# First two chunks of a gated delta rule as one pair with raw keys, two-bank PSUM tiles moved whole, squares summed on ScalarE

## The chip, the cores and the metric

The kernel runs on one core of one Trainium2 chip. The metric is the device time of one execution in microseconds. The core has TensorE (PE, with weight loads listed apart as PEld), VectorE (DVE), ScalarE (ACT), GpSimd (POOL) and SyncE (SP), each with its own queue of instructions, worked off in order; they wait for one another by semaphores.

## The reference

A gated delta rule over 768 time steps for 4 batches x 8 heads with head size 48, and then a dense layer pair with softplus between:

```python
k_n = k / (np.linalg.norm(k, axis=-1, keepdims=True) + 1e-06)
for t in range(S):                                   # state: B, H, 48, 48
    readout = np.einsum('bhd,bhde->bhe', q[:, :, t], state)
    y[:, :, t] = g[:, :, t] * readout
    v_old = np.einsum('bhde,bhd->bhe', state, kt)
    state = state + bt[:, :, :, None] * np.einsum('bhd,bhe->bhde', kt, vt - v_old)
...
x = y.transpose(0, 2, 1, 3).reshape(3072, 384)
h = x @ w_in                                         # 384 -> 2048
g = np.maximum(h, 0.0) + np.log1p(np.exp(-np.abs(h)))
return g @ w_out                                     # 2048 -> 384
```

## The kernel before

The 768 steps are cut into 12 chunks of 64. Within a chunk the recurrence becomes matrix products of 64 x 64 blocks for each of the 32 batch-head pairs: a triangular system in the chunk's keys is inverted, and the states follow from chunk to chunk.

*Items and order.* The kernel does not issue instructions as it goes. It records items (a kind, a chunk, the engines that may run it, what it needs, which tiles it uses) and then emits them in an order written out as a table, `_ORDER`: a word such as `D171` puts item 171 on VectorE. A tile of a ring is taken when the first item that uses it is emitted, and freed after the last. So the table fixes the order on every engine and in SyncE's queue of loads and stores, and it fixes which buffer a chunk gets.

*Stages of a chunk.*
- `norms`: squares of the keys (line 346), their sums by a reduction on VectorE (line 352), the root (ScalarE up to chunk 2, POOL's power after that, line 363), the added 1e-6 and the reciprocal. Chunk 0 is *raw*: its keys go on without being scaled, and the norm is put into beta (`lbeta`) and into v (line 783) instead.
- `front`: keys scaled (`kmul`, line 396) or cast, transposed on TensorE (line 412), evicted (`kev`), queries likewise (line 444, `qev`), then the products of keys with keys and queries (`gram`, line 506). Each comes out in two PSUM banks, m = 0 and 1; four instructions take it out: `kkc` (keys, through the helper of lines 209 and 213) and `mask` (line 488).
- `inverse`: for a group of chunks. Groups are chunk 0, chunk 1, and then pairs. A transpose of 32 x 32 blocks (lines 560 and 565), fifteen elimination steps of two small instructions each (lines 611 and 618) on VectorE or POOL, scalings by the mask of a pair (`ca`, `cb`), transposes back (line 661 for a pair, 665 for one chunk), `tx` (a swap of partition halves) and three products with evictions between (lines 691, 715, 736: `xs`, `td2`, `z`).
- `chain`: old state times keys (`ks`, line 773), v minus that (`w`, line 804), product with the inverse (`umm`, line 818, evicted as `u1`), a second product (`zu`, line 831, `u2`), the new state (`smm`, line 848, `s` at 862), outputs (`qs`, `ymm` line 874, `y` line 888), and a transpose into `xt`.
- `dense`: line 927 makes h in PSUM (two tiles), line 939 takes softplus on ScalarE, line 954 multiplies with w_out, `o` copies out, stores follow. These stand between the chunk stages on TensorE.

Filler matmuls (line 984) on the identity stand in gaps at the start. The PSUM rings are `d` (five single banks), `h` (two) and `o` (one):

```python
r_w = ring("w16", 3, [P, H, D], F16)
r_u = ring("u16", 6, [P, H, D], F16)
r_s = ring("s16", 5, [P, H, D], F16)
p_d = ring("d", 5, [P, 512], F32, psum)
p_h = ring("h", 2, [P, 512], F32, psum)
p_o = ring("o", 1, [P, 512], F32, psum)
```

A stage that makes two banks takes two `d` tiles; one item each takes them out, on ScalarE or VectorE as the table says.

## Time and profile before

| what | us |
|---|---|
| median of 3 runs | 252.6 (252.19 to 253.89) |
| the profiled execution | 250.61 |
| its span, first to last instruction | 248.9 |
| TensorE busy | 219.2 (88%) |
| VectorE busy | 173.0 (69%) |
| ScalarE busy | 160.0 (64%) |
| POOL busy | 107.7 (43%) |

The profile is of one execution. A row of a group gives the line, engine, operation, tiles (written <- read) and shapes, how often, the busy time, the mean of one in ns, and the idle time of the engine ahead of it with what ended it. In the view by windows, each engine has its busy time in that stretch and in brackets its instructions, then come the granted TensorE clock, the DMA share and the traffic. A row of the timeline gives start, duration, engine, line and operation, and in square brackets an idle time and what ended it.

### The profile page before, as it was taken

Reading aid. Unit: us, or ns where it says so; the run is one execution under the profiler, and the core shown is the slowest. Engines: PE = TensorE matmul, PEld = TensorE weight load, DVE = VectorE, ACT = ScalarE, POOL = GpSimd, SP = SyncE. Lnnn points to the kernel's source line nnn. Section 1 sums busy time; section 2 is a strip of 40 time slices with the busy share of each in tenths; the row PEclk is TensorE's granted clock in tenths of the full one; section 3 lists DMA queues with packets and bytes.
Section 4 is the critical chain, followed back from the end, with each engine's and each line's share of the span. In section 5 each row is a group of like instructions: output and inputs, shape, how many; then the busy total and the mean of one; then the engine's idle time right before and its main releaser. Section 6 shows DMA issues by size and latency. Waiting matters only on the chain.

```text
span 248.9 us, 11162 instructions
## 1 busy us (share of the span) xinstructions
PE 219.2 (88%) x4880; PEld 136.6 (55%) x4880; DVE 173.0 (69%) x414; ACT 160.0 (64%) x305; POOL 107.7 (43%) x183
## 2 busy tenths in 40 slices
PE   7666059857998998999999999999999999999993
PEld 2243055644775665455765566655566455677751
DVE  3969999964599987997899989988887233711000
ACT  7675668854596788998668677466672665235540
POOL 8546999662286827858769353303110000000000
PEclk9799657996899999999999999999999999999999
DMA  7999899999996379630999221498300430022013
GB/s 104 185 238 167 115 201 154 203 185 183 208 154 121 71 142 181 169 63 6 172 168 152 41 69 37 91 151 130 66 22 18 97 85 13 5 48 49 18 48 95
DMA packets 86832, 27.55 MB, mean 111 GB/s; under 512 B 77056, under 2 KB 86784, under 8 KB 86784
## 3 DMA queue, kind: packets, MB, share of 16 engines
q1 hardware_dynamic: 81824, 22.31, 52.8%
q0 software_dynamic: 3840, 3.16, 8.6%
q10 hardware_dynamic: 1120, 1.38, 2.2%
q8 instruction: 38, 0.62, 1.1%
q14 instruction: 10, 0.08, 0.2%
HBM read 25.26 MB, written 4.72 MB: 120 GB/s over the span
## 4 chain that ended last, share of the span: by engine, by line
PE 68%; DVE 12%; issue 6%; ACT 6%; DMA 3%; POOL 2%; SPq 1%; POOLq 0%; DVEq 0%; ACTq 0%
PE o L954 25%; PE h L927 21%; PE d L773 3%; ACT kqt L209 2%; PE d L874 2%; PE d L506 2%; PE d L818 2%; DVE tt L618 2%; PE d L444 2%; PE d L831 2%; DMA f<-in_k_dram 2%; DVE tmp L611 2%; DVE mt L488 2%; DVE nv L352 2%; DMA f<-in_q_dram 2%
## 5 line engine op out<-in xcount | busy, mean ns | idle before, releaser
L954 PE MATMUL o<-w_out,ga 128*128 128x384 f16 x384 | 78.3, 329 | 1.1 <-ACT osb L209 0.6
L927 PE MATMUL h<-xt,w_in 128*128 128x512 f16 (+1 forms) x384 | 75.1, 331 | 0.6 <-ACT ga L939 0.5
L939 ACT ACTIVATE ga<-h 128x512 f16<-128x512 f32 x96 | 56.9, 600 | 28.7 <-PE h L927 26.3
L927 PEld LDWEIGHTS <-w_in 128*128 128x128 f16 x384 | 35.5, 99 | 21.6 <-issue 1.1
L954 PEld LDWEIGHTS <-ga 128*128 128x128 f16 x384 | 33.8, 98 | 21.7 <-issue 2.0
L611 POOL TENSOR_TENSOR tmp<-nn,tt 128x78 f32<-128x78 f32 (+7 forms) x57 | 21.5, 377 | 37.2 <-DVE tt L618 32.3
L363 POOL TENSOR_TENSOR nv<-nv,half_c 128x16 f32<-128x16 f32 x9 | 26.3, 2920 | 2.2 <-DVE nv L352 2.2
L618 POOL TENSOR_TENSOR tt<-tt,tmp 128x78 f32<-128x78 f32 (+7 forms) x57 | 20.5, 360 | 4.5
L209 ACT ACTIVATE kqt<-d 128x1024 f16<-128x1024 f16 (+1 forms) x21 | 19.1, 945 | 4.3 <-PE d L412 2.1
L396 POOL TENSOR_TENSOR kn<-f,nv 128x768 f16<-128x768 f32 (+1 forms) x10 | 14.4, 1445 | 13.2 <-PE d L848 6.9
L209 ACT ACTIVATE u<-d 128x384 f16<-128x384 f32 x31 | 14.3, 491 | 9.0 <-PE d L818 4.4
L488 DVE TENSOR_TENSOR mt<-d,mask 128x256 f16<-128x256 f32 x48 | 18.3, 412 | 1.9 <-ACT kk L209 1.0
L209 ACT ACTIVATE osb<-o 128x384 f32<-128x384 f32 x20 | 9.8, 490 | 14.0 <-PE o L954 13.6
L506 PE MATMUL d<-kqt 48*64 48x128 f16 (+1 forms) x448 | 11.3, 217 | 6.7 <-ACT kqt L209 3.2
L888 DVE TENSOR_TENSOR yg<-d,f 128x384 f16<-128x384 f32 x24 | 12.3, 548 | 5.6 <-PE d L874 5.4
L211 DVE CAST u<-d 128x384 f16<-128x384 f32 x17 | 9.3, 554 | 9.3 <-PE d L818 6.6
L984 PE MATMUL h<-ident 128*128 128x512 f16 x40 | 14.0, 513 | 1.7 <-DVE ident L197 1.7
L804 DVE TENSOR_TENSOR w<-f,d 128x384 f16<-128x384 f32 x22 | 11.8, 546 | 4.0 <-PE d L773 4.0
L618 DVE TENSOR_TENSOR tt<-tt,tmp 128x110 f32<-128x110 f32 (+7 forms) x48 | 13.2, 274 | 1.6
L506 PEld LDWEIGHTS <-kqt 48*64 48x64 f16 x448 | 7.6, 109 | 12.2 <-issue 6.8
L611 DVE TENSOR_TENSOR tmp<-nn,tt 128x110 f32<-128x110 f32 (+7 forms) x48 | 12.9, 269 | 1.7 <-POOL tt L618 0.6
L209 ACT ACTIVATE kk<-d 128x256 f16<-128x256 f32 x37 | 12.3, 385 | 2.7 <-PE d L506 2.3
(115 smaller groups left out, 340.4 us busy)
## 6 DMA issues: line engine op xcount, KB each, us to landing
f<-in_k_dram SPq DMA_DIRECT2D x24, 192.0 KB, 5.9
f<-in_q_dram SPq DMA_DIRECT2D x24, 192.0 KB, 4.7
f<-in_v_dram SPq DMA_DIRECT2D x24, 192.0 KB, 5.8
f<-in_g_dram SPq DMA_DIRECT2D x24, 192.0 KB, 5.3
out_dram<-osb SPq DMA_DIRECT2D x34, 96.0 KB, 2.2
w_in<-in_moe_w_in_dram POOLq DMA_DIRECT2D x4, 384.0 KB, 7.2
w_out<-in_moe_w_out_dram POOLq DMA_DIRECT2D x4, 384.0 KB, 8.1
out_dram<-osb ACTq DMA_DIRECT2D x14, 96.0 KB, 2.5
```

Source lines behind the costliest of these rows:

```text
L209: nc.scalar.activation(o, x, AF.Copy, scale=float(sign))
L363: lambda en: nc.gpsimd.tensor_tensor(nv.ap[:, :NU], nv.ap[:, :NU], half_c[:, :NU], ALU.pow),
L396: ENG[en].tensor_tensor(kn[c].ap[:, sl, :, :D], kf.ap[:, sl], nv.ap[:, :NU].rearrange("p (a h) -> p a h", a=2)[:, sl, :, None] .broadcast_ ...
L488: nc.vector.tensor_tensor(mt[c][m].ap[:, NP * p : NP * p + NP], gb[m].ap.rearrange("p (i b) -> p i b", i=NP)[:, :, n : n + C], mask[:, Non ...
L506: nc.tensor.matmul(gb[m].ap.rearrange("p (i b) -> p i b", i=NP)[HALF[r], i, lo:hi], x[:, :C], x[:, lo:hi],)
L611: ENG[en].tensor_tensor(t, nn.ap[:, :, j : j + 1, j + 1 :].broadcast_to([P, 2, w, n]), tt.ap[:, :, :w, j : j + 1].broadcast_to([P, 2, w, n ...
L618: ENG[en].tensor_tensor(rows, rows, t, ALU.add)
L888: lambda en, m=m: nc.vector.tensor_tensor(heads(yg.ap, m), hd(yp[m].ap), heads(gf.ap, m), ALU.mult),
L927: nc.tensor.matmul(hp.ap[:, n * b : n * b + n], w_in[:, j, f * P : (f + 1) * P], xt.ap[:, j, t0 : t0 + n], start=(j == 0), stop=(j == 2),)
L939: lambda en, hp=hp, o=gb: nc.scalar.activation(o.ap, hp.ap, AF.Softplus),
L954: nc.tensor.matmul(op.ap[:, :DM], b.ap[:, col + c0 : col + c0 + 128], w_out[:, f, :], start=(f == 0), stop=(f == NF - 1),)
L984: nc.tensor.matmul(hp.ap, ident, ident[:, None, :].broadcast_to([P, 4, P]))
```

## The change

- Groups are now pairs throughout: chunks 0 and 1 are the first pair, both with raw keys. `lbeta` takes both norms at once, so one inverse less is run (six in place of seven). v of chunk 0 is scaled as part of `w0`; v of chunk 1 as chunk 0's was.
- Roots of chunks 0 to 3 on ScalarE (before: 0 to 2); where POOL takes the root it also adds 1e-6.
- A `d` tile has two banks, and there are two of them; a new single-bank ring `e` serves the transposes. From chunk 2 on (`N_APART`) one instruction takes both banks out; chunks 0 and 1 keep one for each bank.
- `xs` is cut by column block and not by bank, scales by a per-partition mask value, and may run on ScalarE.
- For chunks 9 and 11 (`SUMMED`) squares and sums are made by sixteen ScalarE instructions with an accumulated output, without the reduction on VectorE. Keys may be scaled on ScalarE by sixteen instructions too; the new order does so for chunk 9.
- The identity in f32 borrows another tile, beta for the first pair is loaded without clearing the tile, and the order is a new one (1140 words in place of 1276).

```diff
-N_RAW = 1
-N_SQRT = 3
+N_RAW = 2
+N_SQRT = 4
 N_SPLIT = 2
-GROUPS = [[0], [1], [2, 3], [4, 5], [6, 7], [8, 9], [10, 11]]
+GROUPS = [[0, 1], [2, 3], [4, 5], [6, 7], [8, 9], [10, 11]]
+N_APART = 2
+SUMMED = (9, 11)
+N_LONE = 2
...
-    p_d = ring("d", 5, [P, 512], F32, psum)
+    p_d = ring("d", 2, [P, 1024], F32, psum)
+    p_e = ring("e", 1, [P, 512], F32, psum)
...
+    def moved(kind, c, tag, engs, fn, deps, bufs, size):
+        cuts = [slice(0, 2)] if c >= N_APART else [slice(0, 1), slice(1, 2)]
+        return [
+            add(kind, tag + (f".{rs.start}" if len(cuts) > 1 else ""), engs,
+                lambda en, rs=rs: fn(en, rs), deps=deps, bufs=bufs,
+                size=size * (rs.stop - rs.start))
+            for rs in cuts]
...
+        def summed(en):
+            for a in range(2):
+                for h in range(H):
+                    nc.scalar.activation(
+                        ksq.ap[:, a, h], kf.ap[:, a, h], AF.Square,
+                        accum_out=nv.ap[:, H * a + h : H * a + h + 1])
+
+        if c in SUMMED:
+            i2 = add("sqa", f"{c}", "A", summed, deps=kl, bufs=[kf, ksq, nv], size=768)
...
+            def root(en):
+                nc.gpsimd.tensor_tensor(nvs(), nvs(), half_c[:, :NU], ALU.pow)
+                nc.gpsimd.tensor_scalar_add(nvs(), nvs(), 1e-6)
...
+                    if en == "A":
+                        for a in range(sl.start, sl.stop):
+                            for h in range(H):
+                                nc.scalar.activation(
+                                    kn[c].ap[:, a, h, :D], kf.ap[:, a, h], AF.Copy,
+                                    scale=nv.ap[:, H * a + h : H * a + h + 1])
+                        return
...
-        a4 = [add("u1", f"{c}.{r}", "AD", lambda en, r=r: copy(en, u1[r].ap, hd(up[r].ap)),
-                  deps=[a3], bufs=[u1[r], up[r]], size=384) for r in range(2)]
+        a4 = moved("u1", c, f"{c}", "AD", lambda en, rs: copy(en, u1.ap[:, rs], hds(up, rs)),
+                   [a3], [u1, up], 384)
```

`kkc`, `mask`, `td2`, `z`, `w`, `u2`, `s` and `y` change in the same way as `u1`.

More of the change, by code (lines that the diff above doesn't have):

```diff
@@ L174 @@
     nc.scalar.activation(dummy, half_c[:, :1], AF.Sqrt)
+    ident32 = r_tmp.tiles[1]
     make_identity(nc, ident32)
-    nc.gpsimd.memset(beta_l[:, :2], 0.0)
     for r in range(2):
@@ L244 @@
         for r_ in (r_kn, r_qn):
-            for t in r_.tiles[n : n + 1]:
+            for t in r_.tiles[n : n + 1] if r_ is r_qn or n > 1 else []:
                 setup[n].append(
@@ L341, in norms @@
         kf, kl = tiles["k", c]
-        ksq, nv = Buf(r_f), Buf(r_nv)
+        ksq = Buf(r_f)
+        if RAW[c] and c % 2:
+            nv = nv_of[c - 1]
+        else:
+            nv = Buf(r_nv)
         def square(en):
@@ L893, in chain @@
         xt = xts[cc]
[L894 removed]
+        ytp = Buf(p_e)
         def ytr(en):
@@ L997 @@
         chain(c)
-    jobs = [[0], [1]] + [[c, c + 1] for c in range(2, NC - 2, 2)] + [[NC - 2], [NC - 1]]
+    jobs = [[c] for c in range(N_LONE)]
+    jobs += [[c, c + 1] for c in range(N_LONE, NC - 2, 2)] + [[NC - 2], [NC - 1]]
     for cs in jobs:
```

459 lines of the change are left out of this document (223 added, 236 removed).

## The prediction

> **What bounds the kernel now.** I read the page first: busy shares, slices of the span, and the chain that ended last.
>
> ```profile
> span 248.9 us, 11162 instructions
> PE 219.2 (88%) x4880; PEld 136.6 (55%) x4880; DVE 173.0 (69%) x414; ACT 160.0 (64%) x305; POOL 107.7 (43%) x183
> PE   7666059857998998999999999999999999999993
> PEclk9799657996899999999999999999999999999999
> PE 68%; DVE 12%; issue 6%; ACT 6%; DMA 3%; POOL 2%; SPq 1%; POOLq 0%; DVEq 0%; ACTq 0%
> ```
>
> TensorE is busy for 88% of the span, and the chain that ended last runs over it for 68%. Its slices hold nines and a few eights from the eleventh on (62 us); what is not full lies ahead of that. So the end is set by how early TensorE is given work without gaps, and then by the work itself, which the change leaves alone (4880 matmuls before and after, ten filler groups among them in both).
>
> To see where the head start is made I cut the span at the first matmul of line 818 (the product with the inverse) of chunks 0, 1, 2, 3, 6 and 11. Every chunk passes there in turn.
>
> ```profile
> core 0: us, PE busy (x) PEld busy (x) DVE busy (x) ACT busy (x) POOL busy (x), PEclk, DMA share, GB/s
> 0.00:35.85 35.85, 20.25 (x292) 11.20 (x296) 27.95 (x82) 24.65 (x46) 25.53 (x55) 0.82 1.06 167
> 35.85:54.20 18.35, 15.07 (x429) 10.83 (x425) 15.67 (x37) 14.49 (x30) 14.43 (x17) 0.88 1.28 180
> 54.20:77.46 23.26, 19.21 (x434) 13.21 (x423) 16.32 (x40) 13.78 (x26) 10.43 (x19) 0.85 1.02 171
> 77.46:90.20 12.74, 11.93 (x383) 8.56 (x384) 12.33 (x28) 9.90 (x20) 9.39 (x8) 1.00 0.68 125
> 90.20:142.01 51.81, 50.38 (x1254) 29.45 (x1257) 45.29 (x102) 40.76 (x79) 34.92 (x57) 1.00 0.68 120
> 142.01:215.40 73.39, 73.39 (x1807) 43.14 (x1810) 52.24 (x125) 43.18 (x83) 12.98 (x29) 1.00 0.35 66
> 215.40:248.90 33.50, 28.98 (x327) 20.24 (x326) 3.16 (x6) 13.26 (x24) 0.00 (x0) 1.00 0.20 48
> ```
>
> The reader sees TensorE 20.3 of 35.9 us busy in the first stage (nine filler groups included), then 15.1 of 18.4, 19.2 of 23.3, 11.9 of 12.7, and from 90.2 us on practically all. VectorE is the fuller engine of the others: 15.7 of 18.4 us in the second stage and 12.3 of 12.7 in the fourth. The change can win in the four stages up to 90.2 us (TensorE idle there: 15.6 + 3.3 + 4.1 + 0.8 = 23.8 us) and hardly after it. I cost each stage as a term; the sum goes against the profiled execution, whose span is 248.9 us in a time of 250.61. The median of the three runs, 252.6, is 2.0 above that, and I carry the difference over to it.
>
> **The change, part by part.** *Two banks moved whole.* From chunk 2 on an eviction of 2 x 256 or 2 x 384 elements becomes one instruction; chunks 0 and 1 keep halves. VectorE goes from 414 instructions to about 301, POOL from 183 to about 176; ScalarE rises, because 48 small ones are added.
>
> ```profile
> L488 DVE TENSOR_TENSOR mt<-d,mask 128x256 f16<-128x256 f32 x48 | 18.3, 412 | 1.9 <-ACT kk L209 1.0
> 23.57 0.74 DVE L488 TENSOR_TENSOR mt<-d,mask 128x256 f16<-128x256 f32 x2
> L888 DVE TENSOR_TENSOR yg<-d,f 128x384 f16<-128x384 f32 x24 | 12.3, 548 | 5.6 <-PE d L874 5.4
> L783 DVE TENSOR_TENSOR f<-f,nv 128x768 f32<-128x768 f32 x1 | 0.9, 939 | 0.0
> L209 ACT ACTIVATE u<-d 128x384 f16<-128x384 f32 x31 | 14.3, 491 | 9.0 <-PE d L818 4.4
> L211 DVE CAST u<-d 128x384 f16<-128x384 f32 x17 | 9.3, 554 | 9.3 <-PE d L818 6.6
> L209 ACT ACTIVATE xt<-d 128x768 f16<-128x768 f16 x9 | 7.3, 809 | 9.0 <-PE d L901 9.0
> ```
>
> On VectorE 256 elements cost 412 ns, 384 cost 548: 1.06 ns an element and about 140 ns fixed. A whole move of 768 is then near 0.95 us (line 783 moves 768 in 939 ns, from SBUF). Two halves in a row cost 1.10, so 0.14 us is saved per pair at most; two masks in a row took 0.74 together at 23.57, not 0.82, so it is nearer 0.06. On ScalarE 768 elements from PSUM took 809 ns against 2 x 491. But where the two halves ran side by side on ScalarE and VectorE (0.49 and 0.55), the whole move takes 0.81 to 0.95: 0.3 us later. In the old order 23 of the 40 pairs of u1, u2, z and td2 of chunks 2 to 11 are split between the two engines. In stages where TensorE has dense work to put between, this costs nothing; that cover is the matmuls of lines 927 and 954. Without it the loss is 23 x 0.3 = 7 us, less 30 serial pairs of w, s and y at 0.07: 5 us.
>
> The Trainium skill speaks against this edit: its page "PSUM — Partial Sum Buffer", section "Specifications (TRN2)", says that ScalarE and VectorE can access PSUM in parallel at full bandwidth as long as their banks differ. The old halves lie in two banks, and the trace agrees (both rows above run at their usual length side by side). By that rule alone the sum below would lose those 5 us and end at the old time; that outcome is a rival below.
>
> *Term A, start to the first product (35.85 us before).* The old kernel inverts chunks 0 and 1 in two runs that share VectorE and POOL; the new one inverts them as a pair, once.
>
> ```profile
> 15.06 0.19 DVE L611 TENSOR_TENSOR tmp<-nn,tt 128x30 f32<-128x30 f32 x1
> 18.16 1.07 DVE L565 STREAM_TRANSPOSE ln<-kk 128x512 uint32<-128x512 uint32 x1 [2.18 <-ACT kk L209]
> 29.19 0.48 DVE L618 TENSOR_TENSOR tt<-tt,tmp 128x30 f32<-128x30 f32 x1
> L560 DVE STREAM_TRANSPOSE ln<-kk 128x1024 uint32<-128x1024 uint32 x5 | 9.6, 1925 | 0.0
> L599 POOL TENSOR_TENSOR nn<-ln,beta_l 128x256 f32<-128x256 f16 x4 | 2.9, 734 | 12.9 <-DVE ln L582 12.9
> L611 DVE TENSOR_TENSOR tmp<-nn,tt 128x110 f32<-128x110 f32 (+7 forms) x48 | 12.9, 269 | 1.7 <-POOL tt L618 0.6
> L618 DVE TENSOR_TENSOR tt<-tt,tmp 128x110 f32<-128x110 f32 (+7 forms) x48 | 13.2, 274 | 1.6
> L611 POOL TENSOR_TENSOR tmp<-nn,tt 128x78 f32<-128x78 f32 (+7 forms) x57 | 21.5, 377 | 37.2 <-DVE tt L618 32.3
> L661 DVE STREAM_TRANSPOSE dn<-ta 128x512 uint32<-128x512 uint32 x5 | 5.4, 1079 | 0.0
> L209 ACT ACTIVATE tx<-tb 64x512 f16<-64x512 f16 x3 | 1.9, 628 | 0.2
> 33.56 0.24 PE L715 MATMUL d<-tb,xs 64*64 64x32 f16 x2
> 35.85 0.64 PE L818 MATMUL d<-w,td 64*64 64x48 f16 x32
> ```
>
> The fifteen steps of chunk 0 went from 15.06 to 29.67, 14.6 us, handing over to POOL and back; chunk 1 was ready for its own transpose only at 18.16. In the new order the first two steps are on POOL and the other thirteen stand together on VectorE: 13 x (269 + 274 ns + 0.06 us between) = 7.8 us. The whole term: keys of both chunks evicted at about 14.2 (chunk 1 is no longer normalised first, so it needs neither root nor reciprocal; bounds 13.0, and 18.2 where chunk 1 stood before), transpose 1.93, pick 0.41 (256 elements on VectorE), the POOL half of the preparation 0.73, two POOL steps of two instructions 1.4 (377 ns is the mean there, the first ones are shorter), thirteen steps 7.8, two scalings 2 x 0.41, two output transposes 2 x 1.08, the swap of halves 0.63, two ScalarE joins 0.8, and from the next product to the one of line 818 as before 2.3 (33.56 to 35.85). That is 33.2. What is queued around it: on POOL the squares of chunk 3 stand ahead of half the swap and wait for keys that are now twentieth among SyncE's loads, with the first weight load moved ahead of them on POOL. Twenty loads of 64 x 16 x 48 floats are 3.9 MB, the weights 0.8 MB; at the 167 GB/s of this stage that is 28 us, a little ahead of the swap at 29.4, so it is hidden, and costs up to 2 us if it isn't. So A is 33.2 (31 to 37), a gain of 2.7.
>
> *Term B, to chunk 1's product (18.35 us before).* VectorE's queue is the bound: new on it here are a sum of squares, two key scalings or evictions and the whole masks of chunks 2 and 3, and the state product of chunk 1 stands behind them all. By the rows the instructions there sum to 18.0 us, before to 16.5. With 0.6 us for waits on whole pairs: 18.35 + 1.5 + 0.6 = 20.4 (18.4 to 22).
>
> *Term C, to chunk 2's product (23.26 us before).*
>
> ```profile
> 57.71 0.25 PE L818 MATMUL d<-w,td 64*64 64x48 f16 x3 [3.10 <-issue]
> 58.03 0.56 DVE L211 CAST u<-d 128x384 f16<-128x384 f32 x1 [2.74 <-PE d L818]
> 74.75 1.45 DVE L211 COPY tx<-tb 64x512 f16<-64x512 f16 x1
> 76.26 0.17 PE L715 MATMUL d<-tx,xs 64*64 64x32 f16 x1 [0.91 <-DVE tx L211]
> L211 POOL COPY tx<-tb 64x512 f16<-64x512 f16 x5 | 3.0, 605 | 8.3 <-DVE tb L661 8.2
> ```
>
> Here TensorE stopped for 3.10 us with 29 of 32 matmuls issued, VectorE stood 2.74 us behind it in its queue, and the steps of the next inverse stood behind VectorE. Later the swap of halves, 1.45 us on VectorE, held TensorE 0.91. The new order lets four steps run ahead of that eviction and puts both halves of the swap on POOL (0.61 each). VectorE's rows sum to 16.2 instead of 18.2. I take 2.0 off for these, 1.0 for the swap, and half of the stop (1.6), since nothing in the change removes its cause: 23.26 - 4.6 = 18.7 (15.5 to 23.3).
>
> *Term D (12.74 before):* VectorE's rows go from 12.4 to 12.1; 12.4 (12 to 14.5).
>
> *Squares by sixteen accumulating instructions, chunks 9 and 11, and chunk 9's keys scaled the same way.*
>
> ```profile
> L358 ACT ACTIVATE nv<-nv 128x16 f32<-128x16 f32 x3 | 0.6, 216 | 1.9 <-DVE nv L352 1.9
> L352 DVE TENSOR_REDUCE nv<-f 128x16 f32<-128x768 f32 x12 | 11.2, 937 | 0.4 <-ACT f L346 0.3
> L939 ACT ACTIVATE ga<-h 128x512 f16<-128x512 f32 x96 | 56.9, 600 | 28.7 <-PE h L927 26.3
> ```
>
> The nearest row is 216 ns for 16 elements; with 48 elements I take 0.22 us each, 3.5 us for a chunk. Below, starts overlapping by 0.1 us would give 1.9; above, I allow 0.45 each, 7.2 us, if the accumulated sum is written by a step of its own. They save VectorE 0.94 each. While they run, evictions and the 600 ns softplus of line 939 wait behind them on ScalarE. The Trainium skill's page "ScalarE: Activation LUTs", section "Rules for kernel authors", budgets about 0.3 us for each ACTIVATE plus 0.83 ns an element, from which I estimate 5.4 us a chunk; by it the sum would be 3 x 1.9 = 6 us longer if all were exposed, and no run here shows an accumulating one yet.
>
> *Term E, from chunk 3's product to the end (158.7 before).* TensorE has 28 dense groups behind it there instead of 29, so 0.8 us more to do. In the stage up to 142 ScalarE gains those 32 small instructions (7 us) and joins that VectorE had, and goes from 40.8 to about 50 of 51.8 us; VectorE falls below 40. I take these as even: 159.5. Below, the idle 1.4 us of that stage and the eights of later slices go: 155; above, the ScalarE rival: 167.
>
> The other edits cost nothing: the root's added constant on POOL lies beside VectorE's steps, and the identity, beta and padding moves are in the first 6 us, while the first keys land; without that cover they are 0.2 to 0.6 us each.
>
> Sum: 33.2 + 20.4 + 18.7 + 12.4 + 159.5 = 244.2, 4.7 under the span. On the median: 252.6 - 4.7 = 247.9.
>
> **The rivals.**
>
> *Whole moves cost what the inverse gains.* The two-engine halves were the faster form. For it: 23 split pairs; only two paired PSUM tiles and one single, where there were five singles, so a product waits for the whole eviction ahead of it. Against: TensorE has no gaps from 90 us on. 5 us back: 252.6 + 0.3 = 252.9, no change.
>
> *ScalarE becomes the bound (slower).* Place: the stage from chunk 3's to chunk 6's product. At 0.45 us an accumulating instruction adds 32 x 0.23 = 7.4 to the 50 us there and 3.7 in the stage before, and softplus, which frees the only two tiles of the first dense product, is late. 57.4 - 51.8 + 3.7 = 9.3 over, less 4.7: 257. It decides from about 0.35 us each (50 + 32 x 0.13 = 54 and 2 before). Against: ScalarE stood at 79% there.
>
> *A larger gain.* The stop of 3.10 doesn't recur, B costs nothing more, and A reaches 31: 4.9 + 6.1 + 0.3 - 0.8 = 10.5 off, 242.1. For it: nothing queued on VectorE in the second stage is longer than before by more than the 1.5 us; against: half of A's gain hangs on keys that land in time.
>
> *The head start isn't made.* The pair waits for both chunks' keys and loads; with keys at 18.2 instead of 14.2, A is 37.2, worse by 1.4, and 4.7 shrinks to 0.7: 251.9.
>
> **How the numbers follow.** Forecast 0.48 (its own range 244 to 250), larger gain 0.17, whole moves 0.12, head start not made 0.08, ScalarE 0.15. About 1% is what a measurement here tells from no change, so faster means under 250.1 and slower over 255.1. The first two give 0.65 faster; the two even ones spread a little to the slow side (0.04): same 0.16, slower 0.19. The range goes from 2 us below the larger gain, since E's lower bound lies 4.5 lower, to short of the slow rival: 240 to 256; beyond each end I leave about one in ten.
>
> **What would show it.** Right: line 818's first matmul at about 33 us; thirteen steps in a row on VectorE in some 8 us; chunk 2's product near 72 and chunk 3's near 85; VectorE's sum near 155 us instead of 173 (its rows sum to 25 us less, some of it overlap), TensorE's near 219; nines in TensorE's slices from the tenth on. Wrong: first product at 36 or later, ScalarE full between 85 and 140 with TensorE waiting for line 939, accumulating instructions over 0.35 us, or TensorE's nines giving way to eights after 90 us, waiting for whole evictions.

## The result, and the profile after

The changed kernel took 268.92 us (median of 4 runs, 267.15 to 269.98) where the kernel before took 252.39: 6.8% longer (ratio 1.068, interval 1.057 to 1.080). Forecast were 247.9 us and a range up to 256. The profiled execution took 268.02 us, its span is 266.3. Here and below medians are of all runs, while ratios leave out slow runs, those more than 1.5% above the fastest of the same kernel.

First the page of the changed kernel, the lines that answer to those of before: busy shares, TensorE's slices, the granted clock, and the chain that ended last.

```profile
span 266.3 us, 11059 instructions
PE 225.9 (85%) x4880; PEld 140.3 (53%) x4880; DVE 159.1 (60%) x302; ACT 165.5 (62%) x349; POOL 106.7 (40%) x175
PE   7565666877797689959969999999999999999993
PEclk9965757979999858988999999999999999999999
PE 50%; DVE 15%; DMA 13%; ACT 8%; issue 4%; POOL 3%; ACTq 2%; SPq 2%; DVEq 0%; POOLq 0%
```

VectorE lost 14 us of busy time (about 18 were forecast), and TensorE has the same 4880 matmuls. But TensorE's share of the last chain fell from 68% to 50%, and its slices show a six at the fourteenth, a five at the eighteenth and a six at the twenty-first, where there were nines and a few eights from the eleventh on. The clock row, all nines from the twelfth slice in the kernel before, now dips from the fourteenth to the sixteenth (8, 5, 8) and at the next two eights. Next the same view by windows, cut at the first matmul of the product with the inverse (line 863 now) of chunks 0, 1, 2, 3, 6 and 11.

```profile
core 0: us, PE busy (x) PEld busy (x) DVE busy (x) ACT busy (x) POOL busy (x), PEclk, DMA share, GB/s
0.00:36.89 36.89, 22.03 (x285) 11.75 (x289) 26.35 (x66) 19.33 (x35) 20.51 (x42) 0.76 1.03 163
36.89:60.95 24.06, 18.90 (x453) 13.37 (x449) 16.86 (x33) 14.52 (x28) 15.71 (x17) 0.80 1.16 175
60.95:80.80 19.85, 15.63 (x458) 11.30 (x446) 14.81 (x35) 13.67 (x26) 7.62 (x14) 1.00 0.64 105
80.80:95.20 14.40, 10.16 (x329) 6.99 (x331) 11.35 (x17) 9.35 (x43) 11.89 (x10) 0.86 0.73 159
95.20:159.00 63.80, 57.88 (x1279) 34.43 (x1278) 45.18 (x82) 51.22 (x122) 35.22 (x59) 0.93 0.62 109
159.00:231.80 72.80, 72.12 (x1798) 42.13 (x1797) 41.27 (x69) 44.30 (x75) 15.71 (x35) 1.00 0.32 62
231.80:266.30 34.50, 29.14 (x327) 20.33 (x326) 3.30 (x5) 13.10 (x23) 0.00 (x0) 0.98 0.19 41
```

| stage | before | forecast | after | miss |
|---|---|---|---|---|
| A, to chunk 0's product | 35.85 | 33.2 | 36.89 | +3.7 |
| B, to chunk 1's | 18.35 | 20.4 | 24.06 | +3.7 |
| C, to chunk 2's | 23.26 | 18.7 | 19.85 | +1.2 |
| D, to chunk 3's | 12.74 | 12.4 | 14.40 | +2.0 |
| E, to the end | 158.70 | 159.5 | 171.10 | +11.6 |

More than half of the miss lies in E, and there between the products of chunks 3 and 6 (63.8 us, 51.8 before). TensorE waits there, and the clock granted to it is 0.93 on average. Where does it wait? These are the rows of its timeline with the four longest waits behind 60 us, and a shorter one behind two of them (start, duration, operation, and in brackets the wait and what ended it).

```profile
67.97 0.49 PE L916 MATMUL d<-u,mt 64*64 64x48 f16 x20 [2.38 <-issue]
68.80 0.81 PE L996 MATMUL o<-w_out,ga 128*128 128x384 f16 x4 [0.33 <-DMA w_out<-in_moe_w_out_dram]
...
90.04 0.44 PE L812 MATMUL d<-s,kqt 48*64 48x48 f16 x32 [1.56 <-DVE mt L528]
91.26 0.23 PE L755 MATMUL d<-tb,xs 64*64 64x32 f16 x2 [0.79 <-ACT kk L212]
...
116.72 0.43 PE L729 MATMUL d<-dn,kk 64*64 64x32 f16 x32 [2.53 <-ACT kk L212]
...
136.57 0.61 PE L458 MATMUL e<-ident,kn 128*128 128x128 f16 x8 [2.55 <-ACT xt L212]
```

And these stand on ScalarE at two of the places: the sixteen square-and-sum instructions of chunk 9 (first and last one) ahead of the eviction `kkc` at 88.67, and the sixteen scalings of chunk 9 with chunk 11's sums behind them (132.11 to 135.82) ahead of `xt`. VectorE's mask at 89.29, for which TensorE's product at 90.04 waited, had itself waited for that `kkc`.

```profile
85.07 0.24 ACT L382 ACTIVATE f<-f 128x48 f32<-128x48 f32 x1
...
88.45 0.24 ACT L382 ACTIVATE f<-f 128x48 f32<-128x48 f32 x1
...
88.67 0.59 ACT L212 ACTIVATE kk<-d 128x512 f16<-128x512 f32 x1
...
89.29 1.29 DVE L528 TENSOR_TENSOR mt<-d,mask 128x512 f16<-128x512 f32 x2 [1.29 <-ACT kk L212]
...
128.51 3.71 ACT L439 ACTIVATE kn<-f,nv 128x48 f16<-128x48 f32 x16
...
135.71 0.80 ACT L212 ACTIVATE xt<-e 128x768 f16<-128x768 f16 x1
```

Behind two of these waits, those at 90.04 and 116.72, stands a stretch at half clock. By windows:

```profile
91.05:101.30 10.25, 9.32 (x224) 6.79 (x224) 5.97 (x13) 6.47 (x10) 5.33 (x10) 0.50 0.95 189
118.40:121.80 3.40, 3.40 (x16) 1.76 (x14) 3.23 (x4) 2.61 (x6) 1.66 (x3) 0.50 0.00 0
```

TensorE is busy for 9.3 of 10.25 us there and does about half of what it does at full clock: a window reads as full and is not. Behind the waits of 2.38 us at 67.97 and 2.55 us at 136.57 the clock stays full. Over the span the clock is at half for some 42 us, and for some 24 us in the kernel before, of which nothing lies between 64 and 248 us.

### The profile page after: what moved, and what is told of

It is laid out like the page before. It is cut to its first block, busy times and chain, and to the rows that moved or that the text cites. A ratio compares the mean times of both kernels' runs of the same rounds, so it can differ in the third digit from the quotient of the medians.

```text
span 266.3 us, 11059 instructions
## 1 busy us (share of the span) xinstructions
PE 225.9 (85%) x4880; PEld 140.3 (53%) x4880; DVE 159.1 (60%) x302; ACT 165.5 (62%) x349; POOL 106.7 (40%) x175
## 4 chain that ended last, share of the span: by engine, by line
PE 50%; DVE 15%; DMA 13%; ACT 8%; issue 4%; POOL 3%; ACTq 2%; SPq 2%; DVEq 0%; POOLq 0%
PE o L996 19%; PE h L969 18%; DMA f<-in_k_dram 10%; DMA w_out<-in_moe_w_out_dram 3%; DVE tmp L649 2%; ACTq L1015 2%; DVE mt L528 2%; DVE tt L656 2%; ACT f L382 2%; ACT kk L212 2%; PE d L812 2%; DVE ln L598 1%; DVE yg L930 1%; DVE ta L673 1%; PE d L777 1%
## 5 line engine op out<-in xcount | busy, mean ns | idle before, releaser
L649 POOL TENSOR_TENSOR tmp<-nn,tt 128x30 f32<-128x30 f32 (+7 forms) x43 | 16.0, 371 | 30.2 <-DVE tt L656 26.1
L528 DVE TENSOR_TENSOR mt<-d,mask 128x512 f16<-128x512 f32 (+1 forms) x28 | 16.3, 601 | 11.1 <-ACT kk L212 7.2
L212 ACT ACTIVATE u<-d 128x768 f16<-128x768 f32 (+1 forms) x23 | 16.9, 741 | 9.1 <-PE d L876 4.8
L930 DVE TENSOR_TENSOR yg<-d,f 128x768 f16<-128x768 f32 (+1 forms) x14 | 11.6, 840 | 16.1 <-PE d L916 15.3
L212 ACT ACTIVATE kqt<-e 128x1024 f16<-128x1024 f16 x17 | 17.4, 1023 | 2.7 <-PE e L490 2.1
L212 ACT ACTIVATE kk<-d 128x512 f16<-128x512 f32 (+1 forms) x23 | 12.0, 541 | 10.1 <-DVE mt L528 6.9
L649 DVE TENSOR_TENSOR tmp<-nn,tt 128x96 f32<-128x96 f32 (+7 forms) x47 | 13.1, 278 | 8.5 <-POOL tt L656 7.3
L656 POOL TENSOR_TENSOR tt<-tt,tmp 128x30 f32<-128x30 f32 (+7 forms) x43 | 15.6, 362 | 3.4
L656 DVE TENSOR_TENSOR tt<-tt,tmp 128x96 f32<-128x96 f32 (+7 forms) x47 | 12.5, 267 | 1.6
L598 DVE STREAM_TRANSPOSE ln<-kk 128x1024 uint32<-128x1024 uint32 x6 | 11.5, 1917 | 1.7 <-ACT kk L212 1.7
```

The costliest lines, as they stand in the source:

```text
L212: nc.scalar.activation(o, x, AF.Copy, scale=float(sign))
L528: nc.vector.tensor_tensor(o, banks(gb, ms).rearrange("p m (i b) -> p m i b", i=NP)[:, :, :, n : n + C], mask[:, None, None, :].broadcast_t ...
L598: nc.vector.transpose(o.rearrange("p (w n) -> p w n", w=nw), i.rearrange("p (n w) -> p w n", w=48)[:, 16:],)
L649: ENG[en].tensor_tensor(t, nn.ap[:, :, j : j + 1, j + 1 :].broadcast_to([P, 2, w, n]), tt.ap[:, :, :w, j : j + 1].broadcast_to([P, 2, w, n ...
L656: ENG[en].tensor_tensor(rows, rows, t, ALU.add)
L930: lambda en, ms: nc.vector.tensor_tensor(heads(yg.ap, ms), hds(yp, ms), heads(gf.ap, ms), ALU.mult),
```

## The experiments

Theories to tell apart: the sixteens hold ScalarE (by their place in its queue, or by their work); whole moves of two banks are slower than halves; the last weights come late; the start loses to POOL; TensorE's half clock is a loss of its own, or only a mark of waits. The runs under one heading share a chip and runs of the kernel before, whose median is 249.0 to 251.0 us (the last two runs of the last heading were made apart, on another chip). The changed kernel was not run again beside them; the variants that came out at 268 to 269 us serve as its stand-in under the first two headings.

### One part each

*No sixteens.* Squares of chunks 9 and 11 by one instruction and a reduction on VectorE, chunk 9's keys scaled on VectorE.

```diff
-SUMMED = (9, 11)
+SUMMED = ()
 in the order:
-  ScalarE: sqa 9, kmul 9.0, sqa 11
+  ScalarE: ksq 9, ksq 11;  VectorE: red 9, kmul 9.0, red 11
```

> The changed kernel with the sums of squares of chunks 9 and 11 as one ScalarE square and a VectorE reduction again, and chunk 9's keys scaled by one VectorE instruction; the order is otherwise that of the change. Theory 1 (runs of sixteen hold ScalarE, 3.7 us at 85 us and 7.3 us together at 128 us, and what waits behind them stalls TensorE, whose clock is halved after it): 268.9 falls to 260 to 264, the TensorE gaps before the state product of chunk 3 (1.56 us) and before chunk 9's transposes (2.55 us) go, and the half clock from 91 to 101 us too. Theory 2 (whole moves of two banks: the eviction of keys waits for the mask on the same banks): 267 or more. Theory 3 (the new order brings weights and keys late): 267 or more.

263.9 us (four runs: 259.7, 262.1, 265.7 and 268.5), ratio 1.048 (1.035 to 1.062) from the two shorter ones. The wait of 2.55 us ahead of chunk 9's transposes is gone, the 1.56 us ahead of `ks 3` shrank to 0.54 and 0.47 in two places, and no half clock follows:

```profile
93.90:119.50 25.60, 21.58 (x495) 13.30 (x496) 21.03 (x35) 20.16 (x35) 14.14 (x29) 1.00 0.76 133
```

These 48 instructions cost some 5 to 8 us where the change has them: 5 by the medians, 8 by the two shorter runs against the 269.33 us of the next run on the same chip. By the profiles it is 1.6 us of stage D (12.8 instead of 14.4) and 4.4 of the stage between the products of chunks 3 and 6 (59.4 instead of 63.8). The wait ahead of `xmm 4` stayed at 2.52 us, here with full clock behind it.

*Halves.* All moves of chunks 2 to 11 one bank each, on the same engine, one after the other, in the new order.

```diff
-N_APART = 2
+N_APART = 12
```

> The changed kernel with every move of two banks cut in two instructions again (one for each bank), both on the engine and at the place that the new order gives the whole one. Theory 2: ScalarE can take a bank while VectorE masks the other, the 14 us that the two waited for each other (7.2 and 6.9) halve, and TensorE's 2.53 us gap before chunk 4's first inverse product shrinks: 268.9 falls to 261 to 265, although VectorE and ScalarE get some 109 instructions more. Theories 1 and 3: no gain, 268 to 273, because 109 instructions at 0.06 us each more are put on the two engines.

269.33 us, ratio 1.082 (1.074 to 1.091). No gain: in this order, and with these tiles, cutting the moves is no repair.

*Weights early.* The two last pieces of w_out are loaded ahead of `kmul 4.0` in POOL's queue, not behind it.

```diff
 POOL:
+  wload w1.2, wload w1.3
   kmul 4.0
   ...
-  wload w1.2 ... wload w1.3
```

> The changed kernel with the third and fourth load of the second weights (issued at 55.2 and 60.0 us by POOL, the fourth landed at 68.8) moved ahead of POOL's key scaling of chunk 4, into the time from 51 to 54 us in which POOL waits anyway. Theory 3: the gap of TensorE between 65.6 and 68.8 us (2.38 us that no semaphore explains, then 0.33 for the load) closes, and 268.9 falls by 3 to 5 to 264 to 266. If the 2.38 us are the fetch of instructions and not the weights, it falls by 0.3 to 1. Theories 1 and 2: 268 or more.

265.56 us (265.2 to 266.3), some 3 us under the halves and the next run on the same chip. Stage C falls from 19.85 to 18.3 us; the wait for w_out is gone, and the stop of 2.38 us ahead of `ymm 1`, which nothing in the trace releases, is 0.72.

*Start on ScalarE.* Casts of q0 and q2 and the squares of chunk 3's keys from POOL to ScalarE.

> The changed kernel with the casts of queries 0 and 2 and the squares of keys 3 on ScalarE instead of POOL, at the same places of the order. Theory 4 (POOL's long instructions hold up VectorE's beside them: the 16 elements of chunk 0's norm took 2.64 us at 11.75 us while POOL ran without a pause to 14.36, and elimination step 12 took 2.14 instead of 0.47 beside POOL's squares): these two fall to 0.2 and 0.5 us, the first product of line 863 comes at 33 to 35 us instead of 36.9, and 268.9 falls by 1 to 4. If later waits set the time anyway: umm of chunk 0 earlier, the end within 1 us of 268.9. Theories 1 to 3 say nothing on the start.

268.39 us, no gain. The first inverse's last step did end 2.4 us sooner (28.05 against 30.48), but ScalarE had been given something to wait for, and its query casts, which TensorE needed, stood behind it:

```profile
27.17 0.84 ACT L370 ACTIVATE f<-f 128x768 f32<-128x768 f32 x1 [7.63 <-DMA f<-in_k_dram]
```

### Place, clock and banks

*Fillers in the waits.* Thirteen more filler groups on TensorE, ahead of `ymm 1` (2), `smm 2`, `ks 3` (2), `tmm 3`, `umm 3`, `xmm 4` (3) and chunk 9's transposes (3).

> The changed kernel with thirteen more filler matmul items on TensorE, none of its own work moved: three ahead of xmm 4 and of the key transposes of chunk 9, two ahead of ks 3 and of ymm 1, one ahead of tmm 3, umm 3 and smm 2, that is in the places where its trace shows TensorE waiting 0.7 to 2.6 us. Clock theory: the half clock at 91.05 to 101.3 and at 118.4 to 121.8 costs 13.6 / 2 = 6.8 us, and follows from the thin stretches ahead of it; with them filled it does not come, the stage from chunk 3's to chunk 6's product falls from 63.8 to about 58, and the time from 268.9 to 263. Gap theory: only the waits themselves cost, the clock matters little since TensorE waits for others there; then 268 to 271, the fillers being pure load where a wait is shorter than they are (0.85 us each at full clock).

269.13 us. The half clock at 91 us is gone, and the time is not better. Two rows by windows (the clock is 1.00 in the first) and one of the timeline:

```profile
81.20:94.80 13.60, 13.34 (x348) 7.79 (x351) 10.56 (x15) 9.42 (x43) 11.90 (x10) 1.00 0.76 158
94.80:125.90 31.10, 26.67 (x504) 14.64 (x507) 20.70 (x34) 20.70 (x35) 17.74 (x32) 0.89 0.60 108
```

```profile
115.55 1.86 PE L1026 MATMUL h<-ident 128*128 128x512 f16 x4 [3.63 <-ACT ga L981]
```

The fillers ahead of `xmm 4` need one of the two tiles that softplus reads, waited 3.63 us for it and drew a half clock behind them. The time came out as the gap theory had it. In this stretch a filler is load; what it displaces must be weighed against what it saves.

*Sixteens later.* Chunk 9's sums behind the squares of chunk 8, chunk 11's behind `xt 4`; the scalings stay.

> The sixteens stay on ScalarE, but not ahead of what TensorE waits for: those of chunk 9's sums stand behind the squares of chunk 8 instead of ahead of the eviction kkc 5.0, with the power and the added constant of chunk 9 later too; those of chunk 11's sums stand behind the eviction xt 4 instead of ahead of it. Place theory: the loss of 5 us that the run without sixteens took away came from the place in ScalarE's queue; the two waits of TensorE at 88.5 (1.56 us) and 134 (2.55 us) shrink below 0.8 and the time is 263.5 to 265.5. Work theory: 7 us more on ScalarE in a stage where it is the fuller engine must be paid wherever they stand; then 267 to 270, with softplus late behind them.

266.48 us, half of what removing them gave. Both theories missed: the wait at 134 went, another of 2.71 us came (ahead of `zu 5`, for `u1 5`, now behind the sums).

*Start, second try.* The same casts on ScalarE, the squares of chunk 3 behind the scalings `cb 0.0`.

> Casts of the queries of chunks 0 and 2 and the squares of chunk 3's keys on ScalarE instead of POOL, those squares behind the scalings cb 0.0 of the first inverse (in the earlier run they stood ahead of the query casts and held ScalarE until the keys of chunk 3 had landed, 19.5 to 27.2 us). Theory of the start: VectorE's two small instructions that took 2.64 and 2.14 us beside a busy POOL (about 0.5 each without) are the miss of the first stage; the first inverse's last step then ends at 28.0 instead of 30.5 and chunk 0's product comes at 34.5 instead of 36.9, and the time is 266 to 267. Rival: the weights and keys of later chunks bind, the first product is at 34.5 but chunk 3's is again at 95, and the time is 268 to 269.

266.02 us (263.6 to 267.5); chunk 0's product at 34.2 instead of 36.9, chunk 3's again at 95.3. The time is the theory's and the place of chunk 3's product the rival's; the profile is of the longest of the four runs. First the changed kernel's rows at the two places, then those of this run.

```profile
11.75 2.66 DVE L410 TENSOR_SCALAR nv<-nv 128x16 f32<-128x16 f32 x2
...
27.32 1.38 DVE L649 TENSOR_TENSOR tmp<-nn,tt 128x78 f32<-128x78 f32 x1
28.74 0.76 DVE L656 TENSOR_TENSOR tt<-tt,tmp 128x78 f32<-128x78 f32 x1
...
12.29 1.61 POOL L214 CAST qn<-f 128x768 f16<-128x768 f32 x2
...
27.05 1.56 POOL L372 TENSOR_TENSOR f<-f 128x768 f32<-128x768 f32 x1 [5.93 <-DMA f<-in_k_dram]
28.57 0.83 POOL L843 TENSOR_TENSOR w<-f,nv 128x384 f16<-128x384 f32 x1
```

```profile
11.68 1.06 DVE L410 TENSOR_SCALAR nv<-nv 128x16 f32<-128x16 f32 x2
...
26.35 0.24 DVE L649 TENSOR_TENSOR tmp<-nn,tt 128x78 f32<-128x78 f32 x1
26.62 0.24 DVE L656 TENSOR_TENSOR tt<-tt,tmp 128x78 f32<-128x78 f32 x1
```

Two instructions on 16 elements took 2.66 us while POOL cast queries, and 1.06 with that work on ScalarE; one elimination step took 2.14 us beside POOL's squares and 0.5 without. Together these rows are 3.3 us of stage A's miss of 3.7; the stage itself became 2.7 us shorter. In the profiled run that gain was then lost: B took 25.9 us at a mean clock of 0.64.

*Banks apart.* Only `kkc` and `mask` as halves, 13 of 20 pairs with ScalarE on one bank while VectorE has the other.

```diff
-        cuts = [slice(0, 2)] if c >= N_APART else ...
+        cuts = [slice(0, 2)] if c >= N_APART and kind not in ("kkc", "mask") else ...
 per pair: kkc bank 0 (ScalarE), mask bank 1 (VectorE), then kkc bank 1, mask bank 0
```

> The evictions kkc and mask of chunks 2 to 11 one bank each again, thirteen of twenty pairs arranged so that ScalarE takes one bank while VectorE takes the other, then the other way round (as the kernel before did); all other moves whole. Theory that whole moves make the two engines stand in line for one pair of banks (14 us of waits between these two lines, 1 before): the pair tiles come free 0.6 us sooner each time, TensorE's waits at 53 to 55, 88 to 91 and 114 to 117 shrink by 2 us in all, and the time is 265 to 267. Rival: those waits of the evictions are not on the path, or what the second instruction costs (0.15 us a move) eats it: 268 to 270.

276.06 us: worse by 7, outside both forecasts. The wait ahead of `xmm 4` stayed 2.56, that ahead of `ks 3` rose to 1.95. So neither form of halves mends anything in this order. Why it is so much worse I didn't settle; new waits, 1.92 us ahead of `xmm 2` and 1.21 ahead of `ks 7`, show that the rearranged queues were late in more places.

### Dense work ahead, all repairs, and the early clock

*Dense work ahead.* Work of TensorE's own in place of fillers.

```diff
 TensorE:
+  g2 1.0.12 (from behind ytr 2)
   ks 3
+  g2 1.1.0  (from behind trs k6.0)
   umm 3
+  g2 1.1.12 (from behind g1 2.5)
   xmm 4
```

> The changed kernel with three groups of dense work moved ahead on TensorE, into its waits: the group g2 1.0.12 ahead of ks 3, g2 1.1.0 ahead of umm 3, g2 1.1.12 ahead of xmm 4. Nothing added (the earlier run put fillers there, and had as much more to do as it saved). Theory that thin stretches cost twice, as wait and as the half clock behind them: the waits at 88 to 95 fall by about 1.5 us, the half clock at 91 to 101 is gone or shorter by 3.4 to 6.8 us, xmm 4 follows its inverse at 113 to 114, and the time is 263 to 266. Rival, the inverse's steps set that stage whatever TensorE does: xmm 4 again at 116 to 117 and the time 267 to 269.

266.13 us (263.6 to 268.5). The wait ahead of `ks 3` fell from 1.56 to 0.80, that ahead of `xmm 4` to 1.89, and the half clock of 10.25 us at 91 to 3.4. The time is just over the theory's range, with a scatter that leaves the size open.

*All repairs* (no sixteens, weights early, start, dense work ahead, `cb 4.1` on ScalarE) *and all repairs with five fillers* ahead of `tmm 0`, `zmm 0`, `ymm 0`, `ytr 0` and `gramq 1.0`.

> All four repairs at once: no sixteens (squares and a reduction, chunk 9's keys scaled on VectorE), the two last pieces of the weights loaded ahead of kmul 4.0, the start's casts and the squares of chunk 3 on ScalarE, the three dense groups ahead; and the scaling cb 4.1 on ScalarE beside VectorE's two. Additive theory: 268.9 - 5 - 3.3 - 2.9 - 2 = 255.7 (254 to 258), still 4 to 6 over the kernel before, since the second stage (24 us against 18.4) is not mended. Rival, the repairs mend the same wait (each gives slack that the next can't use): 259 to 263.

> The kernel with all four repairs, and five fillers more on TensorE between 30 and 55 us, ahead of tmm 0, zmm 0, ymm 0, ytr 0 and gramq 1.0, in waits of 0.7 to 1.5 us. Clock theory of the second stage: the half clock that stands there after the start's waits (18.7 us of it from 34 to 60 in the run with the repaired start) falls to under 10, and the time is 2 to 4 us under that of the kernel with the repairs alone. Rival: VectorE's queue sets that stage, TensorE only follows, and the time is the same within 1.

259.83 us (259.45 to 260.13), ratio 1.042 (1.034 to 1.049), without the fillers; 254.23 us (253.87 to 255.06), ratio 1.020 (1.012 to 1.027), with them. The repairs are not additive (255.7 was worked out), as the rival had it: 4 us are missing, of which 1.8 came back in stage B (25.9 against 24.06). Five fillers took 5.6 us off, more than either forecast. Stages B, C and the one up to chunk 6's product by windows, without the fillers and then with them:

```profile
34.60:60.50 25.90, 21.47 (x457) 15.03 (x453) 16.92 (x33) 14.61 (x28) 15.69 (x17) 0.64 1.22 183
60.50:77.60 17.10, 15.61 (x455) 11.12 (x442) 14.64 (x34) 13.63 (x26) 7.67 (x14) 1.00 0.71 123
90.40:151.30 60.90, 54.91 (x1275) 32.68 (x1275) 46.79 (x86) 44.72 (x76) 35.21 (x59) 0.97 0.65 118
```

```profile
34.86:57.40 22.54, 18.27 (x461) 12.14 (x452) 16.60 (x32) 14.48 (x28) 15.96 (x18) 1.00 1.23 196
57.40:74.80 17.40, 15.61 (x444) 11.33 (x445) 14.81 (x36) 13.67 (x26) 7.80 (x14) 1.00 0.73 140
87.60:146.00 58.40, 53.63 (x1279) 32.08 (x1283) 47.06 (x86) 44.81 (x76) 35.21 (x59) 1.00 0.68 124
```

VectorE and ScalarE do the same in both (16.9 and 16.6, 14.6 and 14.5 us in B); the clock is 0.64 in the one and 1.00 in the other, and B is 3.4 us shorter; 2.5 us more come from the last of the three rows. So in B the half clock is a loss of its own, and filling waits of 0.7 to 1.5 us between small products takes it away.

### Whose loss is it?

*Five fillers alone, in the changed kernel.*

> The changed kernel with nothing but the five fillers of the run before (ahead of tmm 0, zmm 0, ymm 0, ytr 0 and gramq 1.0), none of the four repairs. Clock theory: the half clock of the second stage is a loss of its own, whatever stands behind it; the half clock of 33 to 60 is gone, chunk 1's product comes at 57.5 to 58.5 instead of 61, and the time is 263 to 266. Rival: the gain of 5.6 needed the repairs, since VectorE's late inverse and the late weights hold the stages behind; then 267 to 269.

267.22 us (264.0 to 268.0). B falls to 22.4 us and its half clock goes, as the clock theory had it; of the whole the median keeps 1.7 us. In the profile, of the shortest of the four runs, A is 1 us longer and the stage behind chunk 3's product loses its clock as before (63.8 us, mean clock 0.93). The time is the rival's.

*The kernel before, with nine fillers* ahead of `gramq 1.0` (2), `xmm 0` (5), `zmm 0` and `trs q4`.

> The kernel before with nine fillers more in TensorE's waits between 24.6 and 37.2 us: two ahead of gramq 1.0, five ahead of xmm 0, one ahead of zmm 0 and of trs q4. If the half clock at the start costs the old order as much as the new one (13.7 us of it at 26.7 to 40.4, 6.8 at 57.4 to 64.3), this gains 2 to 4 us, 247 to 249, and the fillers are no repair of the change but something that both kernels lacked. Rival: in the old order VectorE and POOL set the pace up to 54 us and TensorE has slack there; then the same within 1, and the new order alone is hurt by the half clock.

253.66 us, ratio 1.021 (1.013 to 1.029): longer by 1 to 3%. In A and B the clock rose and the stages got longer:

```profile
0.00:36.80 36.80, 28.92 (x324) 14.33 (x328) 28.27 (x83) 24.79 (x46) 26.46 (x56) 0.88 1.06 168
36.80:56.60 19.80, 15.02 (x431) 10.93 (x424) 15.71 (x39) 14.45 (x29) 14.41 (x19) 0.97 1.22 173
```

So the half clock did not set these 57 us in the old order. In the same profile C is shorter (20.6 against 23.3 us) and chunk 3's product comes at 89.4, not later than before; the loss lies behind it, where no filler was added, and I can't say what makes it. Both forecasts missed, the rival (no change) by less.

*More dense work ahead,* on top of all repairs and five fillers: `g2 0.1.8` ahead of `zu 1`, `g2 1.0.4` ahead of `smm 2`, `g2 2.0.8` ahead of `ks 5`, `g2 2.0.12` ahead of `zmm 5`.

> The kernel with all repairs and five fillers, and four groups of dense work more moved ahead into waits: g2 0.1.8 ahead of zu 1, g2 1.0.4 ahead of smm 2, g2 2.0.8 ahead of ks 5, g2 2.0.12 ahead of zmm 5 (waits of 0.92, 0.92, 0.49 and 1.06 us). If TensorE is the bound from 57 us on, each wait filled with its own work is gained: 2.5 to 3 us off, 251 to 252. Rival: the waits only move to the next step of the same chain of products; 253.5 to 254.5.

255.59 us, ratio 1.026 (254.23 us and 1.020 without them): no gain, and outside both forecasts. TensorE's waits between 55 and 147 us fell from 9.4 to 7.2 us in all; one grew (`gram 5.1` waited 1.19 us for `y 2` instead of 0.54), and 3.4 us at half clock stand behind it, from 85.5, which the run without the groups does not have. From chunk 1's product to chunk 6's it took 88.7 us, and 88.5 without.

*Sums by sixteens, in three sets of places,* all with the repairs and five fillers: late (behind the squares of chunk 8 and behind `xt 4`, as in *Sixteens later*); where the single squares stand; and there with chunk 9's scalings too, as the change has all 48.

> The kernel with all repairs and five fillers, with the squares of chunks 9 and 11 again by sixteen accumulating instructions, behind the squares of chunk 8 and behind the eviction xt 4 (chunk 9's keys scaled on VectorE). Place theory: where TensorE does not wait behind them they cost nothing, and VectorE is 1.9 us emptier: 253.5 to 255. Work theory: 7.4 us of ScalarE instead of 1.7 us for the two squares holds softplus, which feeds TensorE's dense work, by 1 to 3 us wherever it stands: 255.5 to 258.

> The kernel with all repairs and five fillers (254.2 us), with the squares of chunks 9 and 11 by sixteen accumulating instructions in exactly the places that the single squares have there; chunk 9's keys stay on VectorE. In that kernel's trace ScalarE is idle behind those places, from 79.9 to 82.2 and from 119.0 to 122.2 us, so 3.7 us fit there but for 0.6. Place theory: 253.5 to 255.5 (the run that set them behind xt 4 and behind chunk 8's squares, 259.35, put them where ScalarE had no idle time). Work theory: 257.5 to 260 again.

> The same with chunk 9's keys scaled by sixteen ScalarE instructions too, so that all 48 stand as in the change while the weights, the start, the dense work and the fillers are repaired. Place theory: 48 instructions fit ahead of xt 4 but for about 2 us (116.7 + 3.7 + 3.7 = 124.1 against 122.2), so 255.5 to 257.5, and nearly the whole loss of the change has other causes. Work theory: 259 to 262.

259.35 us (ratio 1.040, 1.034 to 1.046), 255.14 us (1.020, 1.013 to 1.028) and 258.21 us (1.033, 1.025 to 1.041); without any sixteens the ratio is 1.020. The first is above both its forecasts, the second within the place theory's, the third between the two. The waits of TensorE behind them, in the first (two rows, from its longest run, 262.6 us) and the last:

```profile
100.71 1.02 PE L969 MATMUL h<-xt,w_in 128*128 128x512 f16 x4 [1.69 <-ACT ga L981]
...
131.03 0.63 PE L876 MATMUL d<-u,z 64*64 64x48 f16 x32 [2.70 <-ACT u L212]
```

```profile
125.92 0.61 PE L458 MATMUL e<-ident,kn 128*128 128x128 f16 x8 [2.35 <-ACT xt L212]
```

The place decides. The same 32 instructions cost 5 us in the late places and about 1 or less in the old ones, where ScalarE has idle time around them. With the sixteen scalings in front, they hold `xt 4` until 125.1 and TensorE for 2.35, and the whole costs 3 to 4 us. My own choice of a later place was the worse one.

## Why the prediction was wrong

The forecast was 4.7 us less, and 16.5 us more came out. Of the signs of being wrong that it named, two came: the first product after 36 us, and TensorE's nines giving way behind 90 us.

*What was right.* Thirteen elimination steps ran in a row on VectorE (in 9.3 us; 7.8 were forecast, and the step beside POOL's squares alone makes up the rest). Sixteen accumulating instructions take 3.7 us (3.5 forecast). VectorE's busy time fell to 159 us (155 forecast). Stage C gained 3.4 of the 4.6, though the stop of 3.10 us came again, as 2.38. The price of whole moves was put at nothing where dense work covers it; halves in the new order brought nothing back, which leaves the two pair tiles untested.

*The step that failed most: term E, "I take these as even".* It added 7 us of small instructions to ScalarE's 40.8, found 50 of 51.8, and stopped there. ScalarE was busy 51.2 us, as summed, but in 63.8. A sum of busy time says nothing on where in the queue a block of 3.7 us stands, and these blocks stood in front of an eviction that frees one of two pair tiles (88.67) and of the only way out of the single-bank tile (135.71). They are 6 us of the 13.6 that D and E missed together, by the run without them; put in places where ScalarE is idle, 32 of the 48 cost about 1 or less. The rival "ScalarE becomes the bound" had the engine and the stage, but set its point at the price of one instruction (0.35 us each; it was 0.23), so I gave it little. It came in by place, at a price below its own threshold.

By kinds of loss the stage between the products of chunks 3 and 6 comes out so, as an estimate: TensorE's own work in it, each group at its full-clock length, is some 3.5 us more than before (the order moved it there from stages C and D, which hide as much), it is idle for 5.9 us against 1.4, and 9.5 us at half clock lose about 4.8: 12.8, where 12.0 were measured.

*Term E had a second thing wrong: VectorE.* It was to fall below 40 us in that stage and was busy for 45.2, as before (45.3). The wait of 2.53 us ahead of `xmm 4` is not due to ScalarE's blocks, since it stands in the run without them. The eviction that ended it (116.08) had waited for VectorE's mask (115.40), and the mask stood behind three scalings for chunk 4's inverse, drawn out while POOL cast queries and squared keys. The last row is such a scaling with POOL idle.

```profile
111.03 2.52 DVE L673 TENSOR_SCALAR ta<-tt,mx 128x256 f16<-128x256 f32 x2 [0.78 <-POOL tt L656]
113.48 1.05 DVE L673 TENSOR_SCALAR tw<-tt,mx 128x512 f16<-128x512 f32 x1
...
115.40 1.24 DVE L528 TENSOR_TENSOR mt<-d,mask 128x512 f16<-128x512 f32 x2
...
111.72 1.60 POOL L372 TENSOR_TENSOR f<-f 128x768 f32<-128x768 f32 x1
...
116.08 1.20 ACT L212 ACTIVATE kk<-d 128x512 f16<-128x512 f32 x2 [3.22 <-DVE mt L528]
...
73.80 0.43 DVE L673 TENSOR_SCALAR ta<-tt,mx 128x256 f16<-128x256 f32 x1
```

The three took 3.5 us; beside an idle POOL they come to about 1.3 (0.43 each for the first two, 0.48 for the third). It is the same loss as in the start, and no run took POOL's work away here to show its worth; with `cb 4.1` on ScalarE and the dense work ahead the wait is 0.9.

*The clock was not in the sum at all.* The quoted page of before showed it: a PEclk row with sevens, fives and sixes up to the eleventh slice and nines behind. I took "nines from the tenth on" as given, though the change had two tiles to wait for in place of five. In the changed kernel two of the four long waits behind 60 us were followed by 3.4 and 10.2 us at half speed, and the start has more of it (27 us before 61 us).

*Term A* was off by 3.7: keys were ready at 16.3 and not at 14.2, and one step took 2.14. Both are VectorE instructions stretched beside POOL; I had costed them from rows where POOL was idle or elsewhere, while moving the casts onto POOL at that very time. The Trainium skill's "GPSIMD Engine Reference", section "1. Specifications", lists the SBUF interfaces of GpSimd as shared with VectorE, with contention for instructions in a two-port mode or with two SBUF inputs. The trace agrees: 1.38 against 0.24 us for an instruction with two SBUF inputs. I had not looked at POOL's side of the table.

*Term B* was off by 3.7: VectorE was not its bound (16.9 of 24.1 us). TensorE at half clock is 1.7 of it, as the run with five fillers shows (22.4); the other 2 us stay open. *Term D* was off by 2.0: the wait of 1.56 us is for a mask held behind the sixteens; without these D is 12.8. *Term C* missed 1.2: the last weights, issued at 59.99 by a POOL that was busy with keys, and there at 68.8; I had counted the weight load only where it was moved ahead. With the weights early C is 18.3.

*What stays open.* All repairs and the five fillers took 14.7 us off; the new order is then still 2.0% behind (254.23 against 250.57 us), and the 4.7 us that were to be won are missing too. By the profiles it wins 1 us in A and 5.9 in C, and loses 4.2 in B and 6.6 between the products of chunks 3 and 6. Whether that is the two pair tiles in place of five single ones, as the rival of whole moves had it, was not tried: the new order would need other tiles to run on five.

## What to carry to other kernels

Costing a moved instruction by its engine's busy sum is not enough: name the instruction behind it in that queue, and who waits for it. A block of many small instructions is one long instruction to those behind it; the same 32 cost 5 us in one place and about 1 or less in another. Look at what POOL does beside a VectorE instruction before costing it from a row. Where one engine is the bound, read its granted clock with its busy share: a new wait can cost twice, as wait and as the half clock behind it, though only two of four did here. Filling waits took 5.6 us off one version, 1.7 off another, and made the kernel before 1 to 3% longer, so try it before counting on it.

## What the runs showed of the hardware

An accumulating ACTIVATE is two records: the instruction and a read of the accumulator. The view of the line:

```profile
L382 ACT ACTIVATE f<-f x32: 235/238/244, 85.1 to 135.5; 128x48 f32<-128x48 f32 x32
L382 ACT ACTIVATION_READ_ACCUMULATOR f<-f x32: 195/198/203, 85.2 to 135.6; 128x1 f32 x32
```

They overlap with their neighbours, so that a pair passes every 0.23 us; the busy sum (32 x 0.44 = 14 us for two chunks) is about twice the time that the engine is held. The sixteen scalings without an accumulator, 0.33 us each by their records, also follow at 0.23.

Inside the span the half clock came in lengths of 3.4, 6.8, 10.2, 13.7 and 17.1 us. The Trainium skill's "TensorE: Matmul & The Clock Gate", section "What's actually happening", gives a window of 3413 ns and full clock after a busy one. The lengths, multiples of it, bear that out, and in the changed kernel TensorE was busy for 3.2 to 3.4 us of the last window of each half-clock stretch. In the same section the Trainium skill lets the clock fall after an idle window. Here it fell at 91.05 though TensorE had been busy for 1.28 of the 3.41 us before, with waits of 1.56 and 0.79, and at 118.36 after 1.42 of 3.41. The windows with the waits at 67.97 and 136.57 had 1.8 to 2.3 us busy, and the clock stayed full. The border is not sharp: over all runs the clock fell after windows of up to 2.1 us busy, and stayed full after some of 1.5.

TensorE's stops that the profile calls issue have their places in its stream of matmuls, whatever is computed there. The 3.10 us of the kernel before stand ahead of its 736th matmul and the 2.38 us of the changed one ahead of its 863rd. The kernel before with nine fillers stops ahead of its 608th, 736th and 864th, two of these the places where it stops without them. Behind the first 400 matmuls, every such stop of over 0.3 us in all the traces has a number that lies 95 or 96 above a multiple of 128. What happens there the traces don't show; with the weights loaded early the stop at the 863rd is 0.72 us.
